# Handing out the late scaling and turning of attention weights by the gates of the expert stage

## The chip, the cores and the metric

The kernel runs on one core of one Trainium2 chip. The metric is the device time of one execution in microseconds. The engines are TensorE (PE, matrix products; PEld, its weight loads), VectorE (DVE), ScalarE (ACT), GpSimd (POOL) and SyncE (SP), which here only issues transfers (DMA). Each engine works through its own queue in order and waits by semaphores for the others.

## The reference

Attention over 8 batches of 8 heads with 576 positions of 64 elements, masked by blocks of 64, and then an expert layer over the 4608 positions. All of it is in 32-bit floats.

```python
scores = (1 / sqrt(64)) * q @ k.T                 # per batch and head, 576 x 576
scores = where(pos_i // 64 >= pos_j // 64, scores, -1e9)
attn = exp(scores - max(scores))
attn = attn / (sum(attn) + 1e-9)
x = (attn @ v)            # heads side by side: 4608 x 512
h = x @ w_in                                      # 512 -> 2048
g = h * sigmoid(1.702 * h)
out = g @ w_out                                   # 2048 -> 512
```

## The kernel before

**Attention by pairs.** Two heads are worked on together; there are 32 such pairs (`NPAIR`), numbered `n`, four to a batch. The 576 queries of a pair are cut into five chunks, `i` = 0 to 4: chunk 0 has 64 queries, the others 128, and chunk `i` sees `64 * (2i + 1)` keys, which is its `width`. For a chunk TensorE makes the scores, VectorE masks them and takes the row's extreme while copying them out (`weigh`, line 439), ScalarE takes the exponential with the sum beside it (line 446). Then come two steps that this change is about:

- **Scaling** (`normalise`): VectorE adds to the sum and takes the reciprocal (lines 455 and 460), and GpSimd multiplies the weights `e` of each of the two heads with it (line 467). In late pairs chunks 0 to 3 are scaled on GpSimd, two operations each, and chunk 4 on VectorE (line 469).
- **Turning** (`turn`): the weights must be transposed before they are multiplied with the values. VectorE transposes them in blocks of 32 x 32 into one half, `tw`, of the tile `turned`: for each head of chunks 1 to 4 one large operation (line 476), and one small one of 64 partitions for every chunk, 0 too (line 481). After chunk 4, sixteen transfers (line 488, issued by SyncE, outer loop over key blocks `kb`, inner over query blocks `qb`) move the blocks to their places in the other half, `pw`. Each reads one key block of `tw`; the small turns write key blocks 0 and 1 only, the large ones all four.

The values product of a pair (`av`, 60 matrix products `bank<-turned,vp`) reads `pw`.

**The expert stage** works on tiles of 384 positions, 12 of them, with 16 steps each. A step is a *gate*: twelve matrix products into a bank `hp`, a tanh on ScalarE (line 677), g from it on VectorE (line 678), its rounded high part gh on ScalarE (line 686), and the rest gl on GpSimd (line 687, recorded by the helper at line 88). The products of gh and gl with the second weights, nine into banks `acc`, are issued one gate later on TensorE, so that the chain g, gh, gl has the time of a gate and a half. At the last gate of a tile, the next tile is split into high and low parts first (`split`).

**The order of the work.** Pairs 8 to 31 are *late*: their attention runs between gates. `ORDER` writes out the items of a pair; after each item `advance` issues as many gates as a quota by position asks for (`TILES_BY`), and stops at a gate. In a late pair of the plain kind the items come out so on TensorE, with six gates that the text calls A to F:

```
scores of chunks 0-3 | A | N | B | T | C | D | V: values product of the pair before, scores of chunk 4 | E | F
```

At `N` all scaling of chunks 0 to 3 is put into the program, in the order 3, 0, 1, 2, and at `T` all turning. Behind the values product (`av`, line 564) `settle` puts in the weights of chunk 4, then `prep` of the next pair (VectorE turns its queries and keys, line 323, `qt` and `raw`; ScalarE and GpSimd split them into `high` and `low`), and then chunk 4's own scaling and turning.

Matrix products stay in program order. On the other engines, the scheduler may move an operation ahead of ones put in before it: it orders them by priority, which follows the program, among those that it expects to be ready by its own estimate of times. g, gh and gl have a higher priority (`high_priority`). `tc.keep_in_program_order(x)` pins `x` behind the operation put in before it on its engine: it may come later, not earlier.

Buffers tie the chain together. Chunks 0, 1, 2 share one buffer with chunk 4 (`e0`), chunk 3 shares one with `qt` of `prep` (`e1`), so turning them has to end before those can be written. Late gates swap between two banks, and the first scores of a pair borrow the spare one (`lent_bank`), which the g of the gate before the last, E, has to have read.

Of the kernel before, what the change touches and what calls it, by code (L numbers as in the profile page):

```python
# [25 lines left out]
ORDER = (  # L26
# [3 lines left out]
)  # L30

START = "1+0 - B 2/3 L C - V - 4 - a - - -"
HANDOVER = "B C - 0+3/2+1 - - N - T - V - L - - -"
FIRST_LATE = "0+3/2+1 - - N - - T - - V - - -"


WEIGHTS_BY = ((0, 0), (8, 13), (14.5, 32))
# [4 lines left out]
def attention_moe_kernel(  # L42
# [30 lines left out]
    def f(ap):  # L73
        return ap.bitcast(F32)
# [112 lines left out]
    def width(i):  # L187
        return BLK * (2 * i + 1)
# [202 lines left out]
    def settle(n, banks, todo):  # L391
        for chunks, part in zip(banks, todo):
            e = {}
            for i, hd, lo, hi, s in part:
                if i not in e:
                    e[i] = es[i] if early(n) else weights_of(n, i)
                weigh(n, i, hd, lo, hi, s, e[i])
            if early(n):
                for i in chunks[::-1]:
                    if n == 2 * HP - 1 and i == NCH - 1:  # L400
                        with tc.high_priority(offset=300):
                            normalise(n, i, e[i])
                    else:
                        normalise(n, i, e[i])
            else:
                weighed.extend((n, i, e[i]) for i in chunks[::-1])
            if 4 in chunks and not early(n):
                if n + 1 < NPAIR and n != 2 * HP:
                    prep(n + 1)
                normalise_all()  # L410
                turn_all()

    weighed = []
    shared = {}

    def weights_of(n, i):
# [3 lines left out]
            shared[n] = d2.tile([P, 2, S], F32, tag="e0", name="e", bufs=1)  # L420
        return shared[n][:, :, BLK * i * i : BLK * (i + 1) * (i + 1)]

    def normalise_all():
        for x in weighed:
            normalise(*x)

    def turn_all():
        for x in weighed:
            turn(*x)
        weighed.clear()  # L430

    def weigh(n, i, hd, lo, hi, s, e):
        mx, sm = stats[n]
# [14 lines left out]
                bias=mx[0:m, i, hd : hd + 1], accum_out=sm[0:m, i, hd : hd + 1],  # L448
            )

    def normalise(n, i, e):
        _, sm = stats[n]
        m = BLK if i == 0 else P
        c = sm[0:m, i]
        x = nc.vector.tensor_scalar(  # L455
            out=c, in0=c, scalar1=1e-9, scalar2=2.0, op0=ALU.add, op1=ALU.mult
        )
        if not early(n) and i == NCH - 1:
            tc.keep_in_program_order(x)
        nc.vector.reciprocal(out=c, in_=c)  # L460
        on = SCALE_ON[phase(n)][i]
        for hd in range(2):
            x, sc = e[0:m, hd], c[:, hd : hd + 1]
            if n == 2 * HP - 1 and i == NCH - 1:
                on = "DP"[hd]
            if on == "P":
                nc.gpsimd.tensor_tensor(out=x, in0=x, in1=sc.to_broadcast([m, width(i)]), op=ALU.mult)  # L467
            elif on == "D":
                nc.vector.tensor_scalar(out=x, in0=x, scalar1=sc, scalar2=None, op0=ALU.mult)
            else:  # L470
                nc.scalar.activation(out=x, in_=x, func=AF.Copy, scale=sc)

    def turn(n, i, e):

        for hd in range(2 if i else 0):
            nc.vector.transpose(
                out=tw[:, :, SLOT[i] : SLOT[i] + i, hd].rearrange("p b j c -> p j b c"),
                in_=e[:, hd, 0 : i * P],
            )
        r = slice(BLK, P) if i else slice(0, BLK)  # L480
        nc.vector.transpose(  # L481
            out=tw[r, 0:2, 9 + max(i, 1)].rearrange("p b h c -> p h b c"), in_=e[r, :, i * P : width(i)]
        )
        if i == NCH - 1:
            for kb in range(4):
                for qb in range(4):
                    ns = 10 if kb > 1 else NS if qb > 1 else 11
                    nc.sync.dma_start(
                        out=pw[kb * 32 : kb * 32 + 32, qb, 0:ns], in_=tw[qb * 32 : qb * 32 + 32, kb, 0:ns]
                    )  # L490
# [84 lines left out]
    def step(n):  # L575

        turns["n"] = n
        now = n < NPAIR

        def item(x):  # L580
            if x == "V":
                return (lambda: av(n - 1)) if n else None
            if x in ("N", "T"):
                return normalise_all if x == "N" else turn_all
            if x == "L":
                return (lambda: prep(n + 1)) if n + 1 < NPAIR else None
            if x in ("a", "B", "C"):
                m, chunks = {"a": (n, [0, 1]), "B": (n - 1, [2, 3]), "C": (n - 1, [4])}[x]
                return (lambda: flip(m, chunks)) if m >= 0 else None
            return (lambda: score(n, [[int(z) for z in y.split("+")] for y in x.split("/")])) if now and x != "-" else None  # L590

        return [item(x) for x in order(n)]
# [29 lines left out]
    def moe():  # L622
        prev = None

        def second(state):
            g_hi, g_lo, fc, acc, t = state
            todo = [(c, ga, wb) for c in range(TILES[t][1] // P) for ga, wb in ((g_hi, "woh"), (g_hi, "wol"), (g_lo, "woh"))]
            if fc < NFC - 1:

                todo.sort(key=lambda x: (fc == 0 and x[0] == 2, x[1] is g_lo))  # L630
            elif t == NT - 1:
                todo.sort(key=lambda x: (x[0] == 2, x[1] is g_lo))
            begun = set()
            for x, (c, ga, wb) in enumerate(todo):
                last = ga is g_lo
                mm(
                    out=acc[c], lhsT=ga[:, c * P : (c + 1) * P], rhs=weights(wb, fc // FG)[:, fc % FG],
                    start=fc == 0 and c not in begun, stop=fc == NFC - 1 and last,
                )
                begun.add(c)  # L640
                if fc == NFC - 1 and last:
                    osb = out_room([P, DM], F32, "osb", t == NT - 1)
                    nc.scalar.copy(out=osb, in_=acc[c])  # L643
                    r = TILES[t][0] + c * P
                    tc.keep_in_program_order(nc.scalar.dma_start(out=out[r : r + P, :], in_=osb))  # L645
                if x % 3 == 2:
                    yield 650

        for t in range(NT):
            tt = TILES[t][1]  # L650
            if t == 0:
                yield ("tile", 0)
                split(0)
            xh, xl = xs["xh"], xs["xl"]
            acc = [ps.tile([P, DM], F32, tag=f"acc{c}", name=f"acc{c}") for c in range(tt // P)]
            for fc in range(NFC):
                if t == 0:
                    convert(fc // FG * GROUP + NDC + fc % FG + 1)
                hp = next_hp()
                fs = slice(fc % FG * P, (fc % FG + 1) * P)  # L660
                terms = [(wa, xb, dc) for dc in range(NDC) for wa, xb in (("wih", xh), ("wil", xh), ("wih", xl))]
                if fc == 0:

                    terms.sort(key=lambda x: x[1] is xl)
                for cnt, (wa, xb, dc) in enumerate(terms):
                    mm(
                        out=hp[:, 0:tt], lhsT=weights(wa, fc // FG)[:, dc, fs], rhs=xb[:, dc, 0:tt],
                        start=cnt == 0, stop=cnt == 3 * NDC - 1,
                    )
                    if cnt % 3 == 2:  # L670
                        yield unit1(tt)
                g = d2.tile([P, TT], F32, tag="g", name="g", bufs=1)[:, 0:tt]
                gh = d2.tile([P, TT], F32R, tag="gh", name="gh")[:, 0:tt]
                gl = d2.tile([P, TT], F32R, tag="gl", name="gl")[:, 0:tt]

                with tc.high_priority(offset=300):
                    nc.scalar.activation(out=g, in_=hp[:, 0:tt], func=AF.Tanh, scale=1.702)  # L677
                    nc.vector.scalar_tensor_tensor(  # L678
                        out=g, in0=g, scalar=1.0, in1=hp[:, 0:tt], op0=ALU.add, op1=ALU.mult
                    )  # L680

                if fc == NFC - 1 and t + 1 < NT:
                    yield ("tile", t + 1)
                    split(t + 1)
                with tc.high_priority(offset=300):
                    nc.scalar.copy(out=gh, in_=g)  # L686
                    subtract(nc.gpsimd, gl, g, f(gh))
                yield ("gate", fc)
                if prev is not None:
                    yield from second(prev)  # L690
                prev = (gh, gl, fc, acc, t)
        yield from second(prev)
# [87 lines left out]
```

## Time and profile before

| | |
|---|---|
| median of 3 runs | 1093.65 us (1092.28 to 1094.95) |
| the profiled execution | 1093.34 us, its span 1091.6 us |
| granted TensorE clock, mean | 0.992 |
| TensorE busy | 1054.1 us (97%) |
| VectorE busy | 588.8 us (54%) |
| ScalarE busy | 523.5 us (48%) |
| GpSimd busy | 476.3 us (44%) |

The span runs from the first to the last instruction of the program. Rows of the timeline give the start, the duration, the engine, the line, the operation, the tiles as `out<-in`, the shapes and how many were merged into the row; in brackets stands the engine's idle time before it and what ended that. Rows of the waits give the waiting engine and tile, what it waited for, the idle time in total, how often, and the longest. TensorE's ends are modelled, so its starts say more than its ends.

### The profile page before, as it was taken

The numbers are of one execution on the slowest core, as the hardware profiler recorded it, in microseconds if no ns is written. First come the engines' busy times: TensorE is split into PE (matmuls) and PEld (weight loads), VectorE is DVE, ScalarE is ACT, GpSimd is POOL, SyncE is SP. The second block draws the span as 40 slices with busy tenths as digits, with TensorE's granted clock in tenths as the row PEclk, the third lists the DMA queues.
The fourth block names the chain that finished last, engine by engine and source line by source line (L and its number), as shares of the span: only waits on it lengthen the run. The fifth ranks groups of instructions, "written<-read, shape, count | busy, mean of one in ns | idle before, by whom it ended". The sixth has DMA issues, their size and how long they took to land. (4 is left out here: it accounts for less than half of the span.)

```text
span 1091.6 us, 20662 instructions
## 1 busy us (share of the span) xinstructions
PE 1054.1 (97%) x7236; PEld 924.5 (85%) x7236; DVE 588.8 (54%) x1857; ACT 523.5 (48%) x1367; POOL 476.3 (44%) x600
## 2 busy tenths in 40 slices
PE   5969999999999999999999999999999999999998
PEld 3747777888889888898888888998888888999987
DVE  6786786755654655655555664655555654211111
ACT  6866776533544544534444543443544443322322
POOL 5665565634444444344344443443444343222222
PEclk9979999999999999999999999999999999999999
DMA  8735523333333443333434343333444331200000
GB/s 172 213 91 157 148 64 81 98 70 80 91 82 77 112 92 79 83 83 68 107 79 88 89 106 62 79 89 76 105 97 88 66 85 46 53 29 1 30 1 30
DMA packets 219369, 91.30 MB, mean 84 GB/s; under 512 B 197760, under 2 KB 197760, under 8 KB 219264
## 3 DMA queue, kind: packets, MB, share of 16 engines
q1 hardware_dynamic: 209344, 79.94, 32.4%
q10 hardware_dynamic: 9920, 10.03, 2.6%
q8 instruction: 57, 0.93, 0.4%
q14 instruction: 48, 0.39, 0.1%
HBM read 45.09 MB, written 9.44 MB: 50 GB/s over the span
## 5 line engine op out<-in xcount | busy, mean ns | idle before, releaser
L88 POOL TENSOR_TENSOR gl<-g,gh 128x384 fp32r<-128x384 f32 x192 | 194.5, 1013 | 446.7 <-ACT gh L686 431.7
L678 DVE SCALAR_TENSOR_TENSOR g<-g,hp 128x384 f32<-128x384 f32 x192 | 105.4, 549 | 367.5 <-ACT g L677 367.3
L114 PE MATMUL hp<-xh,wih 128*128 128x384 f32 x768 | 260.8, 340 | 3.1 <-DVE g L678 2.4
L114 PE MATMUL hp<-xh,wil 128*128 128x384 f32 x768 | 258.4, 337 | 0.0
L114 PE MATMUL hp<-xl,wih 128*128 128x384 f32 x768 | 254.5, 338 | 0.1
L114 PE MATMUL acc<-woh,gh 128*128 128x512 f32 x576 | 232.2, 403 | 1.2 <-ACT gh L686 1.0
L114 PE MATMUL acc<-wol,gh 128*128 128x512 f32 x576 | 227.7, 395 | 0.0
L677 ACT ACTIVATE g<-hp 128x384 f32<-128x384 f32 x192 | 93.7, 488 | 253.4 <-PE hp L114 215.8
L686 ACT CAST gh<-g 128x384 fp32r<-128x384 f32 x192 | 98.5, 513 | 166.7 <-DVE g L678 166.3
L114 PE MATMUL acc<-woh,gl 128*128 128x512 f32 x576 | 170.7, 394 | 1.4 <-POOL gl L88 1.2
L114 PEld LDWEIGHTS hp<-xh,wih 128*128 128x128 f32 x768 | 144.4, 188 | 16.1 <-DVE g L678 3.4
L114 PEld LDWEIGHTS hp<-xh,wil 128*128 128x128 f32 x768 | 144.3, 188 | 7.7
L114 PEld LDWEIGHTS hp<-xl,wih 128*128 128x128 f32 x768 | 143.8, 188 | 1.0 <-DVE xl L88 1.0
L446 ACT ACTIVATE e<-e,mx 128x192 f32<-128x192 f32 (+3 forms) x240 | 132.4, 554 | 5.9 <-DVE mx L439 4.4
L114 PEld LDWEIGHTS acc<-woh,gl 128*128 128x128 f32 x576 | 107.5, 188 | 28.5 <-POOL gl L88 4.7
L114 PEld LDWEIGHTS acc<-woh,gh 128*128 128x128 f32 x576 | 108.2, 188 | 24.2 <-ACT gh L686 1.8
L467 POOL TENSOR_TENSOR e<-e,sm 128x448 f32<-128x448 f32 (+1 forms) x192 | 112.3, 612 | 34.8 <-DVE sm L460 22.3
L114 PEld LDWEIGHTS acc<-wol,gh 128*128 128x128 f32 x576 | 108.5, 188 | 17.1 <-issue 0.4
L439 DVE CUSTOM_DVE_ANT_0 e<-bank,mask 128x192 f32<-128x192 f32 (+3 forms) x240 | 93.2, 440 | 6.9 <-PE bank L114 6.7
L114 PEld LDWEIGHTS bank<-turned,vp 128*64 128x64 f32 x1800 | 85.4, 137 | 9.7 <-issue 6.6
L114 PE MATMUL bank<-turned,vp 128*64 128x128 f32 (+1 forms) x1800 | 89.6, 257 | 1.6 <-ACT turned L502 1.6
L455 DVE TENSOR_SCALAR sm<-sm 128x2 f32<-128x2 f32 (+1 forms) x160 | 53.9, 338 | 55.4 <-ACT e L446 49.5
(63 smaller groups left out, 1198.2 us busy)
## 6 DMA issues: line engine op xcount, KB each, us to landing
turned<-turned SPq DMA_DIRECT2D x192, 80.0 KB, 2.1
turned<-turned SPq DMA_DIRECT2D x96, 112.0 KB, 2.2
raw<-in_q_dram SPq DMA_DIRECT2D x128, 72.0 KB, 2.3
out_dram<-osb ACTq DMA_DIRECT2D x36, 256.0 KB, 2.3
raw<-in_k_dram SPq DMA_DIRECT2D x120, 72.0 KB, 2.4
turned<-turned SPq DMA_DIRECT2D x96, 88.0 KB, 2.1
words<-in_moe_w_in_dram SPq DMA_DIRECT2D x16, 512.0 KB, 6.0
vp<-in_v_dram SPq DMA_DIRECT2D x60, 128.0 KB, 2.5
```

The costliest lines, as they stand in the source:

```text
L88: eng.tensor_tensor(out=out, in0=in0, in1=in1, op=ALU.subtract)
L114: return tc.keep_in_program_order(nc.tensor.matmul(**kw))
L439: nc.vector.tensor_tensor_reduce(out=e[0:m, hd, lo:hi], in0=s, in1=mk, op0=ALU.add, op1=ALU.min, scale=-0.125, scalar=3e38 if lo == 0 else ...
L446: nc.scalar.activation(out=e[0:m, hd], in_=e[0:m, hd], func=AF.Exp, scale=-1.0, bias=mx[0:m, i, hd : hd + 1], accum_out=sm[0:m, i, hd : hd ...
L455: x = nc.vector.tensor_scalar(out=c, in0=c, scalar1=1e-9, scalar2=2.0, op0=ALU.add, op1=ALU.mult)
L467: nc.gpsimd.tensor_tensor(out=x, in0=x, in1=sc.to_broadcast([m, width(i)]), op=ALU.mult)
L677: nc.scalar.activation(out=g, in_=hp[:, 0:tt], func=AF.Tanh, scale=1.702)
L678: nc.vector.scalar_tensor_tensor(out=g, in0=g, scalar=1.0, in1=hp[:, 0:tt], op0=ALU.add, op1=ALU.mult)
L686: nc.scalar.copy(out=gh, in_=g)
```

## The change

`N` no longer puts the scaling in; it only allows the next gates to do so. From then on, each gate puts in the scaling of up to two chunks behind its gl (`gate_scales`), pinned on GpSimd, and the next gate puts in the turning of these chunks behind its g (`gate_turns`), pinned on VectorE. `T` is gone. In a plain late pair that gives: gate B scales chunks 3 and 0, gate C turns them and scales 1 and 2, gate D turns these. What is left when chunk 4 is settled is put in there (`finish_all`); that happens in pair 8, where a tile's split has to wait for the values product.

```diff
-    "0+3/2+1 - N - T - - V - - - - -",
+    "0+3/2+1 - N - - - - V - - - - -",
...
-                normalise_all()
-                turn_all()
+                finish_all()
...
+    def pin(ins, behind):
+        if behind:
+            tc.keep_in_program_order(ins)
+
+    def finish_all():
+        pace["left"] = 0
         for x in weighed:
             normalise(*x)
-
-    def turn_all():
-        for x in weighed:
+        for x in scaled + weighed:
             turn(*x)
+        scaled.clear()
         weighed.clear()
+
+    def begin_pace():
+        pace["left"] = len(weighed)
+
+    def gate_turns():
+        for x in scaled:
+            turn(*x, behind=True)
+        scaled.clear()
+
+    def gate_scales():
+        for x in weighed[: min(2, pace["left"])]:
+            normalise(*x, behind=True)
+            weighed.remove(x)
+            scaled.append(x)
+            pace["left"] -= 1
...
-                nc.gpsimd.tensor_tensor(out=x, in0=x, in1=sc.to_broadcast([m, width(i)]), op=ALU.mult)
+                pin(nc.gpsimd.tensor_tensor(out=x, in0=x, in1=sc.to_broadcast([m, width(i)]), op=ALU.mult), behind)
...
-            nc.vector.transpose(
+            pin(nc.vector.transpose(
                 out=tw[:, :, SLOT[i] : SLOT[i] + i, hd].rearrange("p b j c -> p j b c"),
                 in_=e[:, hd, 0 : i * P],
-            )
+            ), behind)
...
-            if x in ("N", "T"):
-                return normalise_all if x == "N" else turn_all
+            if x == "N":
+                return begin_pace
...
+                gate_turns()
                 if fc == NFC - 1 and t + 1 < NT:
                     yield ("tile", t + 1)
                     split(t + 1)
                 with tc.high_priority(offset=300):
                     nc.scalar.copy(out=gh, in_=g)
                     subtract(nc.gpsimd, gl, g, f(gh))
+                gate_scales()
                 yield ("gate", fc)
```

The small turns of line 481 are pinned in the same way, and the orders of the first two late pairs (`HANDOVER`, `FIRST_LATE`) lose their `T` too.

More of the change, by code (lines that the diff above doesn't have):

```diff
@@ L28 @@
     "1+0 - B - 2 - C - 3 L V - a - 4 -",
[1 row of a table removed]
[1 row of a table added]
 )
 START = "1+0 - B 2/3 L C - V - 4 - a - - -"
-HANDOVER = "B C - 0+3/2+1 - - N - T - V - L - - -"
-FIRST_LATE = "0+3/2+1 - - N - - T - - V - - -"
+HANDOVER = "B C - 0+3/2+1 - - N - - - V - L - - -"
+FIRST_LATE = "0+3/2+1 - - N - - - - - V - - -"
 WEIGHTS_BY = ((0, 0), (8, 13), (14.5, 32))
@@ L409, in settle @@
                     prep(n + 1)
-                normalise_all()
-                turn_all()
+                finish_all()
     weighed = []
+    scaled = []
+    pace = {"left": 0}
     shared = {}
@@ L421, in weights_of @@
         return shared[n][:, :, BLK * i * i : BLK * (i + 1) * (i + 1)]
-    def normalise_all():
+    def pin(ins, behind):
[3 more added lines that the diff above has]
+        pace["left"] = 0
         for x in weighed:
             normalise(*x)
-    def turn_all():
-        for x in weighed:
+        for x in scaled + weighed:
             turn(*x)
+        scaled.clear()
         weighed.clear()
+    def begin_pace():
[10 more added lines that the diff above has]
+            pace["left"] -= 1
     def weigh(n, i, hd, lo, hi, s, e):
@@ L449, in weigh, with normalise @@
             )
-    def normalise(n, i, e):
+    def normalise(n, i, e, behind=False):
         _, sm = stats[n]
@@ L471, in normalise, with turn @@
                 nc.scalar.activation(out=x, in_=x, func=AF.Copy, scale=sc)
-    def turn(n, i, e):
+    def turn(n, i, e, behind=False):
         for hd in range(2 if i else 0):
-            nc.vector.transpose(
+            pin(nc.vector.transpose(
                 out=tw[:, :, SLOT[i] : SLOT[i] + i, hd].rearrange("p b j c -> p j b c"),
                 in_=e[:, hd, 0 : i * P],
-            )
+            ), behind)
         r = slice(BLK, P) if i else slice(0, BLK)
-        nc.vector.transpose(
+        pin(nc.vector.transpose(
             out=tw[r, 0:2, 9 + max(i, 1)].rearrange("p b h c -> p h b c"), in_=e[r, :, i * P : width(i)]
-        )
+        ), behind)
         if i == NCH - 1:
```

## The prediction

> **What bounds the kernel now.** I read the page first, then the waits of TensorE alone, then the timelines of VectorE, GpSimd and TensorE over single pairs of the late stage, which the change touches.
>
> ```profile
> span 1091.6 us, 20662 instructions
> PE 1054.1 (97%) x7236; PEld 924.5 (85%) x7236; DVE 588.8 (54%) x1857; ACT 523.5 (48%) x1367; POOL 476.3 (44%) x600
> PE   5969999999999999999999999999999999999998
> ```
>
> TensorE is busy for 97% of the span, and all its loose slices stand at the start and the very end. From about 205 us on it is the path itself, in an order written out by hand; a change to the other engines is worth what TensorE's waits gain or lose. Between 204 and 950 us, all late pairs, the view of waits lists these for it:
>
> ```profile
> PE acc L114 <- POOL gl L88: 1.2, 4, 0.6
> PE acc L114 <- ACT gh L686: 1.0, 1, 1.0
> PE bank L114 <- DVE g L678: 0.9, 2, 0.5
> PE bank L114 <- POOL low L88: 0.2, 1, 0.2
> ```
>
> That is 3.3 us in 746, so the ceiling of any gain is near 0.4%, while there are more than twenty late pairs over which a new wait repeats. So the question is which of the waits go, and which margins are thin. A pair has six gates; I call them A to D (between its scores of chunks 0 to 3 and the values product) and E, F (behind chunk 4's scores). One plain pair on VectorE:
>
> ```profile
> 501.45 0.30 DVE L481 STREAM_TRANSPOSE turned<-e 64x128 f32<-64x128 f32 x1
> ...
> 505.75 0.70 DVE L481 STREAM_TRANSPOSE turned<-e 64x128 f32<-64x128 f32 x3
> 509.36 0.55 DVE L678 SCALAR_TENSOR_TENSOR g<-g,hp 128x384 f32<-128x384 f32 x1 [2.90 <-ACT g L677]
> 509.83 2.07 DVE L476 STREAM_TRANSPOSE turned<-e 128x384 f32<-128x384 f32 x6
> 511.82 0.73 DVE L323 STREAM_TRANSPOSE qt<-raw 128x576 f32<-128x576 f32 x1
> ...
> 513.29 0.52 DVE L439 CUSTOM_DVE_ANT_0 e<-bank,mask 128x384 f32<-128x384 f32 x1
> ...
> 516.85 0.49 DVE L455 TENSOR_SCALAR sm<-sm 128x2 f32<-128x2 f32 x1 [1.60 <-ACT e L446]
> ...
> 519.65 0.52 DVE L678 SCALAR_TENSOR_TENSOR g<-g,hp 128x384 f32<-128x384 f32 x1
> ```
>
> The ten turns of chunks 0 to 3 stand in three places: one small one behind gate B's g (501.45), three small ones behind gate C's (505.75), and the six large ones behind gate D's (509.83). Behind those six comes a chain without slack: the next pair's two transposes (511.82), chunk 4's weights (513.29), the exponentials on ScalarE (the 1.60 of idle before 516.85), chunk 4's scaling and turning, and only then gate E's g at 519.65. The next pair's scores go into the spare gate bank, which that g has to release. Score starts on TensorE, with the g before each where it stands alone:
>
> ```profile
> 521.17 0.24 PE L114 MATMUL bank<-high 64*64 64x64 f32 x2
> 270.27 0.24 PE L114 MATMUL bank<-high 64*64 64x64 f32 x2
> 302.33 0.24 PE L114 MATMUL bank<-high 64*64 64x64 f32 x2 [0.46 <-DVE g L678]
> 552.88 0.24 PE L114 MATMUL bank<-high 64*64 64x64 f32 x2 [0.46 <-DVE g L678]
> 332.00 0.51 DVE L678 SCALAR_TENSOR_TENSOR g<-g,hp 128x384 f32<-128x384 f32 x1
> 333.52 0.24 PE L114 MATMUL bank<-high 64*64 64x64 f32 x2
> 895.27 0.52 DVE L678 SCALAR_TENSOR_TENSOR g<-g,hp 128x384 f32<-128x384 f32 x1
> 896.79 0.24 PE L114 MATMUL bank<-high 64*64 64x64 f32 x2
> 802.16 0.52 DVE L678 SCALAR_TENSOR_TENSOR g<-g,hp 128x384 f32<-128x384 f32 x1
> 802.79 0.24 PE L114 MATMUL bank<-high 64*64 64x64 f32 x2
> ```
>
> The plain pairs, 17 of them from 333.52 to 896.79, have about 1.00 us between the end of gate E's g and the score (521.17 less 519.65 and 0.52; 1.01 and 1.00 in the first and the last). At 802.79 it is 0.11, and at 302.33 and 552.88 nothing is left: TensorE waits there.
>
> **The change part by part.**
>
> *Scaling on GpSimd.* Chunks 3 and 0 are now pinned behind gate B's gl, 1 and 2 behind gate C's. Before, all eight scalings ran as soon as they could, ahead of a gate's gl:
>
> ```profile
> 872.81 2.82 POOL L467 TENSOR_TENSOR e<-e,sm 64x64 f32<-64x64 f32 x6 [0.36 <-DVE sm L455]
> 875.60 1.00 POOL L88 TENSOR_TENSOR gl<-g,gh 128x384 fp32r<-128x384 f32 x1
> 284.89 0.40 PE L114 MATMUL acc<-wol,gh 128*128 128x512 f32 x1
> 285.38 0.50 PE L114 MATMUL acc<-woh,gl 128*128 128x512 f32 x1
> ```
>
> gl starts the moment the six scalings end. Such lateness is behind the four waits for gl (1.2 us idle). TensorE's ends are modelled and overlap the next start by some 0.16 us (a 0.39 us matmul, the next 0.23 later), so by starts they cost 1.2 + 4 x 0.16 = 1.8. At 285.38 a use of gl starts 0.49 behind its forerunner instead of 0.23: 0.26 more; it is bound to a tile's splitting, which scaling on GpSimd slows, and I count it as going. The moved scalings cost nothing: gates B and C lie 4.30 us apart (the turns at 501.45 and 505.75), a gl takes 1.00 of it, and gate B's half of the scaling, 2 x (448 + 64) columns, is an estimated 2.5 us by the 2.82 that 2 x (64 + 192 + 320) columns took; gate C's half is as long. Both fit into the remaining 3.3. If they did not, gate C's gl would be late next, and TensorE first uses that behind the values product.
>
> *The one wait for gh.* The chain of waits names it, in the last late pair:
>
> ```profile
> 905.32 1.37 POOL e L467 x2
> 906.71 0.31 DVE turned L481
> 907.05 0.57 DVE g L678
> ```
>
> A turn queued ahead of gate A's g waited for its scaling. Pinned behind gate C's g it cannot: 1.0 idle, 1.2 by starts. Gains together: 1.8 + 0.3 + 1.2 = 3.3 us.
>
> *Turning on VectorE.* Pins only say "not before". Chunk 3's turns are pinned in a chain (large, large, small) behind gate C's g, chunk 0's small one behind those, chunks 1 and 2 behind gate D's g. Where the large ones go was not set by the program before: they could be placed anywhere behind their scaling, and in every plain pair they stand behind gate D's g, though VectorE idles 2.90 us before it. What holds them is the previous pair's transfers out of the same tile:
>
> ```profile
> 520.01 10.06 SPq L488 DMA_DIRECT2D turned<-turned x16
> ```
>
> A small turn writes only what the first eight of the sixteen transfers read, a large one what all read. So the scheduler, which orders by the times it expects, takes the small ones a gate or two earlier than the large. The change moves no transfer (the sixteen are still issued behind chunk 4's turn, on the same queue behind the same eight loads), so I expect chunk 3's large turns behind gate D's g again, and now all four small ones, being chained behind large ones or pinned behind that g, with them: ten turns at that place instead of six. What that costs, the trace shows once, in the pair whose score starts at 270.27:
>
> ```profile
> 258.45 0.55 DVE L678 SCALAR_TENSOR_TENSOR g<-g,hp 128x384 f32<-128x384 f32 x1 [3.42 <-ACT g L677]
> 259.04 0.70 DVE L481 STREAM_TRANSPOSE turned<-e 64x128 f32<-64x128 f32 x3
> 259.75 2.08 DVE L476 STREAM_TRANSPOSE turned<-e 128x384 f32<-128x384 f32 x6
> ...
> 263.22 0.52 DVE L439 CUSTOM_DVE_ANT_0 e<-bank,mask 128x384 f32<-128x384 f32 x1
> ...
> 269.59 0.52 DVE L678 SCALAR_TENSOR_TENSOR g<-g,hp 128x384 f32<-128x384 f32 x1
> ```
>
> Nine turns: chunk 4's weights start 4.77 behind gate D's g, against 3.93 in the plain pair; gate E's g ends 0.16 before the score, against 1.00. Three small turns cost 0.84, and all of it arrives. Four cost 1.11. Bounds: 0.93 (four at 0.70/3 each) and 1.3 (four at the lone 0.30, and a little for changes of shape).
>
> The Trainium skill, "VectorE: DVE Perf Modes", section "The DRAIN you can't avoid", says that an operation does not start until the one before it has left the pipe. By that, four small turns would cost 4 x 0.30 = 1.20 and the sum below would be 1.9 us worse. The trace does not agree: three take 0.70, less than three times 0.30.
>
> A score waits for what exceeds its room, and for some 0.06 of signalling (room 0.06 was left where TensorE waited: 302.33 less the g's end). Plain pairs: 1.11 - 1.00 + 0.06 = 0.17, times 17 is 2.9. The two that already wait: 1.11 each, 2.2. At 802.79: 1.11 - 0.11 + 0.06 = 1.06. At 270.27 one more turn: 0.28 - 0.16 + 0.06 = 0.18. Together 6.3.
>
> *The handover pair.* There the values product and chunk 4 now come before the scaling in the program, because a tile's split waits for them. The scaling is ready as early as before and chunk 4 needs the same buffer free, so I take nothing; bounds -0.5 and +0.5. Nothing earlier is touched.
>
> *Sum.* 6.3 - 3.3 = +3.0 us on the profiled execution's 1093.34 (0.3 below the median of the runs): 1096.3.
>
> **The rivals.**
>
> *1, faster: the turns go where the program names them.* If the transfers count as finished by gate C's g, chunk 3's three turns and chunk 0's run there, in idle time. Behind gate D's g stand then four large and two small: the two 384-wide ones are half the columns of 1.99 us (509.83 to 511.82), so -1.00 + 0.55 = -0.45. The existing waits shrink by 0.45 each: 1093.34 - 3.3 - 0.9 = 1089.1. For it: VectorE is idle there, and the transfers are issued by 530.07, while the next gate C turns at about 537.0 (505.75 and one pair, which is 563.27 / 18 = 31.3 us from 333.52 to 896.79). Against: the same idle time was open before and no plain pair used it. It decides as soon as the expected landing falls before gate D's g.
>
> *2, faster: the longer row of turns lets chunk 4's weights overtake the transposes.* That order stands once in the trace:
>
> ```profile
> 232.96 0.56 DVE L439 CUSTOM_DVE_ANT_0 e<-bank,mask 128x384 f32<-128x384 f32 x1 [2.50 <-PE bank L114]
> ...
> 233.92 0.77 DVE L323 STREAM_TRANSPOSE raw<-raw 128x576 f32<-128x576 f32 x1
> ```
>
> The weights would start at 511.82 + 1.11 = 512.93, so 0.36 earlier than now: no new wait, the old two 0.36 shorter, 1093.34 - 3.3 - 0.7 = 1089.3. Against: with nine turns the order held.
>
> *3, no change.* The four small turns cost the lower bound, 0.93: plain pairs stay just clear (0 each), 1.9 + 1.0 remain, less 3.3: 1093.
>
> *4, much slower.* A pinned scaling or turn heads its queue before its input is there, once a pair, 0.3 us or more over 20 pairs: 1100. The trace shows the inputs early, so little speaks for it.
>
> **How the numbers follow.** About 0.2%, 2.2 us, is what a measurement of this kernel can tell from no change: below 1091.5 faster, above 1095.8 slower. All ten turns in one place has 0.62, of which 0.42 with the full price (slower) and 0.20 with a price near the lower bound (rival 3, the same). Rival 1 has 0.17, rival 2 0.10, both faster. Rival 4 has 0.06, and 0.05 goes to the terms simply cancelling. So faster 0.27, same 0.25, slower 0.48. The range runs from rivals 1 and 2 to the upper bound of the price: with 1.3 the plain pairs wait 0.36, 6.1 in all, 2.6 + 1.25 + 0.4 for the others, less 3.3 is +7.1, 1100.4. So 1088.8 to 1100.4; the forecast's own range is 1093 to 1100.4.
>
> **What would show it.** Right: GpSimd's gl no longer starts at the end of scalings and TensorE's waits for gl and gh between 204 and 950 us vanish; behind gate D's g stand ten turns; chunk 4's weights start about 5.0 behind that g; TensorE's waits for VectorE's g at the score rise from 2 to about 20, some 0.1 us of idle each and over 1 us in three. Wrong: fewer than ten turns there, or gate E's g ahead of chunk 4's turns; then the wait for g disappears and the kernel gains 3 to 4 us.

## The result, and the profile after

| | before | after |
|---|---|---|
| median of 5 runs | 1093.65 us (1092.28 to 1094.95) | 1111.77 us (1109.39 to 1112.59) |
| span of the profiled execution | 1091.6 us | 1110.0 us |
| TensorE busy | 1054.1 us (97%) | 1059.3 us (95%) |

The change makes the kernel slower: after to before is 1.0163, 95% interval 1.0147 to 1.0179. I had forecast slower, but by 3 us instead of 18, and 1111.77 lies outside my range. From the page of the changed kernel:

```profile
PE 1059.3 (95%) x7236; PEld 927.5 (84%) x7236; DVE 590.2 (53%) x1857; ACT 520.8 (47%) x1367; POOL 477.8 (43%) x600
```

The same instructions are busy for much the same time. TensorE's idle time grew most, from 37.5 to 50.7 us; its busy time grew by 5.2, but its ends are modelled, so the account below goes by its starts. Its waits between 204 and 950 us, the view that carried the prediction (idle in total, times, longest):

```profile
PE bank L114 <- DVE g L702: 14.2, 19, 2.0
PE hp L114 <- ACT xh L635: 2.7, 2, 1.3
PE acc L114 <- ACT osb L667: 1.1, 3, 0.4
```

The waits for gl and gh are gone, as forecast. The wait for gate E's g rose from 0.9 us in 2 places to 14.2 in 19, and two kinds are new. A plain pair on VectorE (in this kernel's lines 500 is the large turn, 505 the small one, 702 is g), then its score on TensorE:

```profile
581.74 0.56 DVE L702 SCALAR_TENSOR_TENSOR g<-g,hp 128x384 f32<-128x384 f32 x1 [3.63 <-ACT g L701]
582.21 1.03 DVE L500 STREAM_TRANSPOSE turned<-e 128x384 f32<-128x384 f32 x2
583.26 0.64 DVE L505 STREAM_TRANSPOSE turned<-e 64x128 f32<-64x128 f32 x2
583.83 0.45 DVE L500 STREAM_TRANSPOSE turned<-e 128x128 f32<-128x128 f32 x2
584.30 0.31 DVE L505 STREAM_TRANSPOSE turned<-e 64x128 f32<-64x128 f32 x1
584.62 0.77 DVE L500 STREAM_TRANSPOSE turned<-e 128x256 f32<-128x256 f32 x2
585.41 0.31 DVE L505 STREAM_TRANSPOSE turned<-e 64x128 f32<-64x128 f32 x1
585.75 0.78 DVE L323 STREAM_TRANSPOSE qt<-raw 128x576 f32<-128x576 f32 x1
586.56 0.78 DVE L323 STREAM_TRANSPOSE raw<-raw 128x576 f32<-128x576 f32 x1
587.26 0.52 DVE L463 CUSTOM_DVE_ANT_0 e<-bank,mask 128x384 f32<-128x384 f32 x1
...
593.64 0.52 DVE L702 SCALAR_TENSOR_TENSOR g<-g,hp 128x384 f32<-128x384 f32 x1
594.21 0.24 PE L114 MATMUL bank<-high 64*64 64x64 f32 x2 [0.58 <-DVE g L702]
```

All ten turns stand behind gate D's g, and VectorE idles 3.63 us before it: the place that I had forecast. Chunk 4's weights start 5.52 behind that g (587.26 less 581.74) where I had put 5.0, and from there to gate E's g it is 6.38, much as before (519.65 less 513.29 is 6.36). In the kernel before, the weights start 3.94 behind g (3.93 by the rounded rows). So four small turns cost 5.52 - 3.94 = 1.58 us, not 1.11. The 20 other pairs from 263 to 910 us show the same: 5.51 to 5.53, and 5.78 in two of them.

For the whole loss I compared, matmul by matmul, how far each start lies behind the one before it with the median of the same pair of operations in the kernel before. Of the 18.4 us between the two spans, +14.5 go to waits for g, +3.0 to waits for xh, +1.6 to waits for osb, -3.1 to the lost waits for gl and gh, +1.6 to matmuls that start late without a listed wait (1.4 of it from 300 to 327 us), and 0.9 to the stage before 200 us, which the change does not touch.

### The profile page after: what moved, and what is told of

Same layout as the page of the kernel before. It is cut to its first block, busy times and chain, and to the rows that moved or that the text cites. A ratio compares the mean times of both kernels' runs of the same rounds, so it can differ in the third digit from the quotient of the medians.

```text
span 1110.0 us, 20531 instructions
## 1 busy us (share of the span) xinstructions
PE 1059.3 (95%) x7236; PEld 927.5 (84%) x7236; DVE 590.2 (53%) x1857; ACT 520.8 (47%) x1367; POOL 477.8 (43%) x600
## 4 chain that ended last, share of the span: by engine, by line
PE 66%; DVE 14%; ACT 10%; DMA 5%; issue 3%; POOL 1%; SPq 0%; DVEq 0%; ACTq 0%; POOLq 0%
PE hp L114 27%; PE acc L114 26%; PE bank L114 12%; DVE turned L500 4%; ACT e L470 3%; DMA vp<-in_v_dram 3%; ACT high L324 2%; DVE e L493 2%; DMA out_dram<-osb 1%; DVE g L702 1%; PE bank L117 1%; DVE sm L479 1%; DVE turned L505 1%; ACT turned L470 1%; DVE xl L88 1%
## 5 line engine op out<-in xcount | busy, mean ns | idle before, releaser
L500 DVE STREAM_TRANSPOSE turned<-e 128x384 f32<-128x384 f32 (+1 forms) x192 | 85.6, 482 | 0.7 <-issue 0.3
```

What stands on the lines that cost most here:

```text
L500: pin(nc.vector.transpose(out=tw[:, :, SLOT[i] : SLOT[i] + i, hd].rearrange("p b j c -> p j b c"), in_=e[:, hd, 0 : i * P],), behind)
```

## The experiments

Each ratio compares a run with runs of the kernel before that were taken beside it; their medians lie between 1092.6 and 1093.85 us.

**Is it the pinning of the turns?**

```diff
# behind the gates, but free to be placed
-            turn(*x, behind=True)
+            turn(*x)
```

> The scaling stays handed out and pinned by the gates; the turning is put in at the same gates but not pinned. Theory (the row of ten turns behind gate D's g): the small turns go back behind gates B and C, six turns stand behind D's g, chunk 4's weights start 3.9 us behind it, TensorE's waits for g at the score fall from 14.2 us in 19 waits to about 1 us in 2, and the time is 1091 to 1093. Rival (the pinned scaling makes the weights late): nothing changes, 1109 or more.

1105.49 us, ratio 1.0116 (1.0101 to 1.0131). My number missed by far, and instructively. VectorE goes back to the old order, six turns behind gate D's g, but now that g is late:

```profile
577.36 0.31 DVE L505 STREAM_TRANSPOSE turned<-e 64x128 f32<-64x128 f32 x1 [1.05 <-POOL e L491]
577.70 0.55 DVE L702 SCALAR_TENSOR_TENSOR g<-g,hp 128x384 f32<-128x384 f32 x1
578.17 2.07 DVE L500 STREAM_TRANSPOSE turned<-e 128x384 f32<-128x384 f32 x6
```

The tanh on ScalarE that this g needs had ended at 576.45 (it starts at 575.96 and takes 0.49). A small turn, placed ahead of g, waits for its scaling, which is now done in two halves behind gl:

```profile
575.00 2.33 POOL L491 TENSOR_TENSOR e<-e,sm 128x192 f32<-128x192 f32 x4
```

That is the form of my fourth rival, in a kernel where the turns are not pinned. TensorE still waits 8.6 us for g, in 18 places. So late scaling has a price of its own, which pinned turns hide: behind g, they can't make it late.

**The scaling free, the turns pinned.**

```diff
-            normalise(*x, behind=True)
+            normalise(*x)
```

> The other half: the scaling is put in by the gates without a pin, the turning stays pinned. Theory: ten turns behind gate D's g, chunk 4's weights 5.5 us behind it, 1110 to 1113. Rival (pinned scaling): the waits for g go, 1096 or less.

1114.98 us, ratio 1.0205 (1.0181 to 1.023).

```profile
PE bank L114 <- DVE g L702: 15.0, 19, 1.9
PE acc L114 <- POOL gl L88: 4.2, 7, 1.0
```

The waits for g stay and the waits for gl come back, more than the 1.2 us of the kernel before. Pinning the scaling is thus worth some 3 us by the medians and 4.6 by the ratios, and the turns carry the loss. This run's times spread the most, from 1112.77 to 1118.42 us.

**Is the place of the small turns enough?** The kernel before, with only its four small turns pinned behind gate D's g (in the order 3, 0, 1, 2, ahead of the six large ones); `gate_smalls` is called behind each gate's g:

```diff
+            turn(*x, part="large" if split else "")
...
+            gates["left"] = 2
...
+    def gate_smalls():
+        gates["left"] -= 1
+        if smalls and gates["left"] == 0:
+            for x in smalls:
+                turn(*x, part="small")
+            smalls.clear()
...
-                return normalise_all if x == "N" else turn_all
+                return normalise_all if x == "N" else (lambda: turn_all(n > 2 * HP))
```

> The kernel before, scaling untouched, with nothing but its four small turns of chunks 0 to 3 pinned behind gate D's g, where they come out as a row of four ahead of the six large ones. Theory: this alone makes the new waits, at the price of a row of four: weights 4.9 to 5.05 us behind gate D's g, 1097 to 1101. If the price is 0.39 for each of them: 5.5 us, 1109 to 1113. If the place of the turns is not the cause: 1093 to 1095.

1107.74 us, ratio 1.0137 (1.012 to 1.0154). A loss of nearly the same size is there without any of the rest, but it is only in part the same: of its waits, 7.6 us are for g, and 4.2 for gl, which the changed kernel has not.

```profile
PE bank L114 <- DVE g L695: 7.6, 18, 1.7
PE acc L114 <- POOL gl L88: 4.2, 7, 1.0
...
580.18 0.55 DVE L695 SCALAR_TENSOR_TENSOR g<-g,hp 128x384 f32<-128x384 f32 x1 [3.63 <-ACT g L694]
580.76 1.15 DVE L496 STREAM_TRANSPOSE turned<-e 64x128 f32<-64x128 f32 x4
...
585.40 0.52 DVE L452 CUSTOM_DVE_ANT_0 e<-bank,mask 128x384 f32<-128x384 f32 x1
```

Here four small turns cost 5.22 - 3.94 = 1.28.

**The same ten turns in another order.** The changed kernel with the six large turns first, then the small ones 3, 2, 1, 0 in a row:

```diff
-            turn(*x, behind=True)
+            turn(*x, behind=True, part="large")
+        smalls.extend(scaled)
...
+        if len(smalls) == 4:
+            for x in sorted(smalls, key=lambda x: -x[1]):
+                turn(*x, behind=True, part="small")
+            smalls.clear()
```

> As the changed kernel, with the same ten turns pinned behind gate D's g, but the six large ones first and the four small ones in a row at the end. If a small turn costs what it costs between others only because the shape changes (0.39 us each in the changed kernel), four in a row cost 0.9 to 1.1 together: chunk 4's weights start 4.9 to 5.05 us behind gate D's g, each plain pair waits 0.1 to 0.2, and the time is 1096 to 1100. If each costs 0.39 anywhere in this row: 5.5 us and 1110 or more.

1099.44 us, ratio 1.0059 (1.0044 to 1.0074): two thirds of the loss are gone, with the same instructions in the same gate.

```profile
574.46 0.55 DVE L711 SCALAR_TENSOR_TENSOR g<-g,hp 128x384 f32<-128x384 f32 x1 [3.63 <-ACT g L710]
...
577.01 1.02 DVE L514 STREAM_TRANSPOSE turned<-e 64x128 f32<-64x128 f32 x4
...
579.42 0.52 DVE L470 CUSTOM_DVE_ANT_0 e<-bank,mask 128x384 f32<-128x384 f32 x1
```

The weights start 4.96 behind g; four small turns cost 1.02. So the price belongs to the order, not to the turn.

**What in the order costs?** Chunk 0's small turn lies on partitions 0 to 63, the others on 64 to 127, and everything else here starts at partition 0. Counting the steps between a start at 0 and a start at 64 gives 2 with the small ones last, 4 with them ahead in the order 3, 0, 1, 2, 6 in the changed kernel, and 2 for the three small turns of the pair at 258.45. The four prices 1.02, 1.28, 1.58 and 0.84 follow, to within 0.04, from 0.19 for a small turn and 0.14 for a step; but these two numbers were fitted to them. The rival is the change between large and small shapes. Two orders on which they differ:

```diff
# first
-            for x in sorted(smalls, key=lambda x: -x[1]):
+            for x in sorted(smalls, key=lambda x: (3, 0, 2, 1).index(x[1])):
# second
-            turn(*x, behind=True, part="large")
-        smalls.extend(scaled)
+            turn(*x, behind=True, part="large" if x[1] else "")
+        smalls.extend(x for x in scaled if x[1])
...
-        if len(smalls) == 4:
+        if len(smalls) == 3:
```

> The six large turns and then the four small ones in a row behind gate D's g, as in the run with the small ones last, but in the order 3, 0, 2, 1 instead of 3, 2, 1, 0. Chunk 0's small turn lies on partitions 0 to 63, the other three on 64 to 127. My theory, fitted to four prices so far (0.84, 1.03, 1.28, 1.58): a small turn costs 0.19, and each step of VectorE from work that starts at partition 0 to work that starts at partition 64, or back, costs 0.14 more. Here there are four such steps (large to 3, 3 to 0, 0 to 2, 1 to qt) instead of two, so 4 x 0.19 + 4 x 0.14 = 1.31: chunk 4's weights 5.25 behind gate D's g instead of 4.97, plain pairs wait about 0.36, and the time lies between the two known ones: 1099.4 + 22 x 0.28 = 1105.6. Rival: the price is that of changing between large and small shapes; that happens twice here as there, so 4.97 and 1099.4.

> As the run with the small turns last, but chunk 0's small turn stands between chunk 3's large ones and chunk 1's, and only 3, 2, 1 are in a row at the end. Steps between partition 0 and partition 64: two, as with all four last (chunk 0's starts at partition 0, as its neighbours do). My theory: 4 x 0.19 + 2 x 0.14 = 1.03, weights of chunk 4 at 4.97 behind gate D's g, 1099.4. Rival, changes of shape: four of them instead of two, 1.31, weights at 5.25, about 1105.6.

The first took 1106.08 us, ratio 1.0102 (1.0082 to 1.0122), the second 1100.12, ratio 1.0052 (1.0038 to 1.0067). VectorE with the order 3, 0, 2, 1:

```profile
577.80 0.56 DVE L711 SCALAR_TENSOR_TENSOR g<-g,hp 128x384 f32<-128x384 f32 x1 [3.64 <-ACT g L710]
...
580.35 1.16 DVE L514 STREAM_TRANSPOSE turned<-e 64x128 f32<-64x128 f32 x4
...
583.06 0.52 DVE L470 CUSTOM_DVE_ANT_0 e<-bank,mask 128x384 f32<-128x384 f32 x1
```

and with chunk 0's small turn among the large ones:

```profile
576.35 0.55 DVE L711 SCALAR_TENSOR_TENSOR g<-g,hp 128x384 f32<-128x384 f32 x1 [3.63 <-ACT g L710]
576.82 1.03 DVE L507 STREAM_TRANSPOSE turned<-e 128x384 f32<-128x384 f32 x2
577.77 0.26 DVE L514 STREAM_TRANSPOSE turned<-e 64x128 f32<-64x128 f32 x1
577.97 1.11 DVE L507 STREAM_TRANSPOSE turned<-e 128x128 f32<-128x128 f32 x4
579.09 0.70 DVE L514 STREAM_TRANSPOSE turned<-e 64x128 f32<-64x128 f32 x3
...
581.33 0.52 DVE L470 CUSTOM_DVE_ANT_0 e<-bank,mask 128x384 f32<-128x384 f32 x1
```

Weights 5.26 and 4.98 behind g, where the steps gave 5.25 and 4.97 and the shapes the reverse. This was forecast, not fitted. The rows show how a step costs. Chunk 0's turn starts at 577.77, 0.08 before the large ones ahead of it end (576.82 + 1.03), and its own follower 0.06 before it ends. In the changed kernel every upper small turn, and what follows it, starts only when the one before has ended: 584.30 behind 583.83 + 0.45, 584.62 behind 584.30 + 0.31, 585.75 behind 585.41 + 0.31.

The Trainium skill, "VectorE: DVE Perf Modes", section "Two Vector instructions with no wait between them", states that an instruction is held until all earlier ones on VectorE have finished when its input or output starts in another group of 32 partitions than the last one in the same memory did. The trace agrees, as the starts above show; the Trainium skill gives no price there, the runs give 0.14 us a step. That section stands right behind the one that I weighed in the prediction, and that one points to it.

**What holds the large turns behind gate D's g?** The loads of the next pair's inputs issued behind the sixteen transfers instead of ahead of them, in the changed kernel (shown; `hold` keeps `prep` from issuing them) and in the one before:

```diff
+                m = None
...
-                    prep(n + 1)
+                    m = prep(n + 1, hold=True)
                 finish_all()
+                if m is not None:
+                    load(m)
```

> The changed kernel, with the next pair's eight loads issued behind the sixteen transfers of the turned weights instead of ahead of them. Theory (these transfers hold chunk 3's large turns behind gate D's g): the transfers end some 4 us earlier, chunk 3's turns and chunk 0's run behind gate C's g as the program names them, six turns stand behind D's g, the waits for g at the score fall below 3 us in all, 1090 to 1096. Rival (something else holds them): ten turns stay, 1110 or more.

> The kernel before with the same move of the eight loads behind the sixteen transfers, nothing else. Theory: the large turns leave the place behind gate D's g for the gate before, chunk 4's weights start up to 2 us earlier behind D's g, the waits for g at 302 and 552 us go, 1090 to 1093. If the loads are late for the next pair's transposes: new waits, over 1096.

1096.94 us, ratio 1.0031 (1.0019 to 1.0043), and 1097.33, ratio 1.0026 (1.0016 to 1.0037), both above the ranges that I had named. In the first, chunk 3's turns now stand behind gate C's g:

```profile
565.45 0.55 DVE L706 SCALAR_TENSOR_TENSOR g<-g,hp 128x384 f32<-128x384 f32 x1 [3.63 <-ACT g L705]
565.92 1.03 DVE L504 STREAM_TRANSPOSE turned<-e 128x384 f32<-128x384 f32 x2
566.97 0.31 DVE L509 STREAM_TRANSPOSE turned<-e 64x128 f32<-64x128 f32 x1
569.64 0.56 DVE L706 SCALAR_TENSOR_TENSOR g<-g,hp 128x384 f32<-128x384 f32 x1 [2.37 <-ACT g L705]
```

So with the sixteen transfers earlier on their queue chunk 3's large turns go a gate earlier, which is what I had argued from their rows. Not everywhere: of the 21 pairs from 262 to 895 us, three keep all ten turns behind gate D's g, nine have seven to nine there, and nine have six. In the kernel before, where no pin holds any turn, three pairs keep all six large ones there too, and in the others some or all go earlier. The next pair's `qt` now comes behind chunk 4's first weights as well, presumably because its inputs are loaded later, and the waits for g vanish. Other waits come in their place (the first kernel's):

```profile
PE acc L114 <- ACT osb L671: 2.6, 2, 1.3
PE bank L114 <- POOL low L88: 1.4, 6, 0.3
```

**All scaling at gate B.** If both the late scaling and the place of the small turns cost, then scaling all four chunks behind gate B's gl and leaving the turns free should avoid both:

```diff
-        for x in weighed[: min(2, pace["left"])]:
+        for x in weighed[: min(4, pace["left"])]:
-            turn(*x, behind=True)
+            turn(*x)
```

> The gates hand out the scaling, but gate B's takes all four chunks, pinned behind its gl, and the turning is put in at gate C without a pin. The run with free turns was slow because the scaling of chunks 1 and 2 ended behind gate D's g; here it ends some 4 us earlier. Theory (whatever delays gate D's g or lengthens the row behind it costs, nothing else): gate D's g is on time, six turns behind it, waits for g as before the change, waits for gl gone but for what the copies of a tile's end then cost: 1090 to 1094. Rival (late scaling costs by itself): 1100 or more.

1088.96 us, ratio 0.9945 (0.9929 to 0.996): faster than both kernels and than the 1090 to 1094 that I had forecast. TensorE's waits from 204 to 950 us are down to two. GpSimd does the eight scalings between two gl. The second gl starts only when they end, 0.9 us behind its gh, but TensorE does not wait for it:

```profile
PE bank L114 <- DVE g L702: 0.4, 1, 0.4
PE bank L114 <- POOL low L88: 0.2, 1, 0.2
...
567.18 0.51 ACT L711 CAST gh<-g 128x384 fp32r<-128x384 f32 x1 [1.13 <-DVE g L702]
564.05 4.61 POOL L491 TENSOR_TENSOR e<-e,sm 128x448 f32<-128x448 f32 x8
568.62 1.01 POOL L88 TENSOR_TENSOR gl<-g,gh 128x384 fp32r<-128x384 f32 x1
```

The later loads on top of this:

> Both: all scaling behind gate B's gl with free turns, and the loads behind the transfers. Theory: no wait for gl, and none for g at the score: 1088 to 1092, the best of these. If the later loads cost: as the run with the loads alone, over 1096.

1096.93 us, ratio 1.0031 (1.0019 to 1.0043). They undo the gain. All three kernels with later loads end at 1097, whatever their turns. Their listed waits of TensorE come to 4.6, 4.4 (the kernel before) and 4.8 us, against 3.3 in the kernel before as it was, but they are not the same ones: osb takes 2.6 in the two changed kernels, gl 3.1 in the other. What sets the common level was not taken apart.

## Why the prediction was wrong

**Right: the mechanism.** The ten turns in one place, the transfers as what holds chunk 3's large ones (in most pairs), the constant way from chunk 4's weights to gate E's g, the score as the place where TensorE waits, and the end of the waits for gl and gh (3.1 us; I had 3.3) all came out. Rivals 1 and 2 did not happen: all ten turns stayed behind gate D's g, and `qt` and `raw` still came before the weights.

**Wrong: "Three small turns cost 0.84 ... Four cost 1.11. Bounds: 0.93 ... and 1.3".** This is the step that failed. I divided one observed row by three and took the quotient for the price of a turn. Two thirds of that row were three turns at 0.19, one third was two steps between partitions, and the new order has six steps. By the same two numbers 4 x 0.19 + 6 x 0.14 = 1.60, against 1.58 measured; my upper bound, "four at the lone 0.30, and a little for changes of shape", let each small turn cost its whole length but not the instruction behind it.

A small error in this term is large in the sum, since the room was 1.0: a plain pair's wait is 0.17 at 1.11, and 0.64 at 1.58. So the waits for g came to 14.5 more, where I had 6.3. With 1.58 in place of 1.11, the working of the prediction gives 17 x 0.64 + 2 x 1.58 + 1.53 + 0.64 = 16.2, so this one term accounts for the miss there. Two smaller slips change little: one of the 17 plain pairs had a room of 0.75, not 1.00 (its g ends at 770.86, its score starts at 771.61), and the lower end of the range, 1088.8, lies below what rival 1 works out to, 1089.1.

**Left out: what is late behind gate E's g.** I priced the lateness only at the score. In the changed kernel the copy out of `acc` at a tile's first gate runs 12.34 us behind the start of gate E's g, the same as in the kernel that scales at gate B (374.43 less 362.10, 12.33). The first three rows are the changed kernel's, the last two that kernel's:

```profile
367.99 0.51 DVE L702 SCALAR_TENSOR_TENSOR g<-g,hp 128x384 f32<-128x384 f32 x1
380.33 0.59 ACT L667 COPY osb<-acc 128x512 f32<-128x512 f32 x1 [1.09 <-DMA out_dram<-osb]
380.96 0.50 PE L114 MATMUL acc<-woh,gh 128*128 128x512 f32 x1 [0.36 <-ACT osb L667]
...
362.10 0.52 DVE L702 SCALAR_TENSOR_TENSOR g<-g,hp 128x384 f32<-128x384 f32 x1
374.43 0.59 ACT L667 COPY osb<-acc 128x512 f32<-128x512 f32 x1 [1.10 <-DMA out_dram<-osb]
```

The copy is no slower. TensorE's score starts 0.57 behind that g's start in the changed kernel (368.56) and 1.51 in the other (363.61). Released by g, TensorE is nearer to the copy, and waits. The waits for xh have the same origin: ScalarE's queue stands before its copies, waiting for the input transposes at the end of the row of turns:

```profile
457.89 0.78 DVE L323 STREAM_TRANSPOSE raw<-raw 128x576 f32<-128x576 f32 x1
458.74 0.67 ACT L324 CAST high<-raw 128x576 fp32r<-128x576 f32 x1 [4.57 <-DVE raw L323]
459.90 0.52 ACT L635 CAST xh<-xr 128x384 fp32r<-128x384 f32 x1
```

With the shorter row of the small turns last, these waits fall from 2.7 to 1.5 us, and with six turns there and the scaling at gate B they are gone. Together xh and osb cost 4.6 us, for which my sum had nothing.

**The rest: the granted clock.** Of the 1.6 us without a listed wait, 1.4 are slower starts from 300 to 327 us, behind a wait of 1.96 us on TensorE (at 303.38). A stretch of the changed kernel there and one of the kernel before (PE, PEld, DVE, ACT and POOL busy, the granted clock, the DMA share, GB/s):

```profile
304.10:307.50 3.40, 3.40 (x20) 2.90 (x17) 1.92 (x9) 1.86 (x5) 1.66 (x2) 0.50 0.53 118
...
265.00:322.00 57.00, 56.45 (x380) 50.32 (x380) 31.87 (x104) 27.93 (x75) 25.73 (x34) 1.00 0.41 92
```

For 3.4 us the granted clock is 0.50, and 1.00 again behind it. Between 204 and 950 us the twelve traces show such a stretch five times, each time 0.5 to 1.4 us behind the end of a wait of TensorE: of 1.96 here, of 1.68 with the small turns ahead, of 1.86 and 1.89 with the scaling free, and of 2.29 with the order 3, 0, 2, 1. One wait of that length was not followed by it (1.81, at 306.44 with the scaling free), and none of the shorter ones was, up to 1.66. So the traces tie the half clock to the long waits that the lost room makes; no run changes such a wait alone.

The 0.9 us before 200 us go with the clock too. The mean granted clock of the first 200 us is 0.96 in the kernel before and 0.94 in the changed one, and the first score of a late pair starts at 205.67 and 206.43. Over all twelve traces that start lies between 204.65 (clock 0.96) and 208.22 (0.93), so 0.9 us is within what this stage varies by.

## What to carry to other kernels

Ask of every observed price what it is made of before multiplying it: here a row of three operations held two prices, one for the operation and one for each change of its place, and only orders with different counts told them apart. Where several operations on half the partitions share a queue with full ones, keep those of one half together. A term that stands against a margin of its own size needs a range wide enough for the margin to fall, and a late engine is then late for everybody behind it, not only at the first wait; and if a pin moves work later, ask which unpinned work ahead of an urgent operation will wait for it.

## What the runs showed of the hardware that I had not expected

A transpose on VectorE that starts at partition 64 does not overlap the end of one that starts at partition 0, nor the other way round: 0.14 us for each step, about three quarters of the small transpose itself (0.19 start to start). A small transpose at partition 0 between large ones paid nothing for its shape.

Behind five of the six waits of TensorE of 1.68 us or more between 204 and 950 us, the granted clock stood at 0.50 for 3.4 us, and behind none of the shorter ones. In the changed kernel that cost about 1.4 us.
